# Sliding-window attention on 32-row array tiles: scores of two heads with 64 keys per tile, full PSUM banks, static probability buffers and a hand-made order of all array work

## The chip, the cores and the metric

One core of one Trainium2 chip runs the whole program. The metric is the device time of one execution in microseconds (us). Every run is compared with runs of the kernel before on the same chip.

Engines: PE is the matmul array (PEld its weight loads), DVE is VectorE, ACT is ScalarE, POOL is GpSimd, SP issues most transfers. Each executes its own list of instructions in order (the VectorE timeline of e6 below shows one standing behind another); semaphores tie them together.

## The reference

Two layers, each an attention block and a feed-forward block with residuals, 2048 rows of 512, 32 heads of 16, a window of 256 keys:

```python
def _A_ref(x, wqkv, wo):
    H = 32; Dh = D // H; W = 256
    # ... q, k, v from x @ wqkv
    scores = jnp.einsum("bhqd,bhkd->bhqk", q, k) * (Dh ** -0.5)
    mask = (idx[:, None] - idx[None, :] >= 0) & (idx[:, None] - idx[None, :] < W)
    p = _softmax(jnp.where(mask, scores, -1e9))
    # ... o = p @ v, then o @ wo
x = x + _A_ref(_layernorm(x), A_wqkv, A_wo)
x = x + _B_ref(_layernorm(x), B_w1, B_w2)    # relu feed-forward, 512 -> 1792 -> 512
# ... and both once more
```

## The kernel before

Rows are worked on in four chunks of 512 per layer. The scheduler of the build orders all instructions by five priority classes (scores first, feed-forward last). Q is isolated per head by transfers into zero-padded tiles, so that one matmul over all 128 rows of K gives the scores of four heads; GpSimd masks, and GpSimd computes the layer-norm rows:

```python
def layer_norm_chunk(c, xnT, sfx, startup=False, j0=0, j1=4):
    # ... statistics on VectorE; rstd by Ln and Exp on ScalarE
    nc.vector.scalar_tensor_tensor(out=nb[:, j0:j1], in0=mv4[:, j0:j1, 0], scalar=-1.0, in1=rstd[:, j0:j1],
                                   op0=ALU.mult, op1=ALU.mult)
    # ... for each of four row blocks
            nc.gpsimd.tensor_scalar(out=xn[:], in0=x_sb[:, b, :], scalar1=rstd[:, j:j + 1],
                                    scalar2=nb[:, j:j + 1], op0=ALU.mult, op1=ALU.add)
            nc.sync.dma_start_transpose(out=xnT[...], in_=xn[...])

# scores of one block of 128 queries with one block of 128 keys, eight heads
for xh in range(2):
    nc.tensor.matmul(Sps[:, xh]..., lhsT=KT[:, t, kcols], rhs=Qih[:, t, 4 * xh:4 * xh + 4, qcols], start=True, stop=True)
nc.scalar.activation(pt[:, kbi]..., Sps[...], ACT.Exp)
# ... two masks on GpSimd (affine_select), then 8 heads x 3 key blocks:
nc.tensor.matmul(acc[:, h % 16, :], lhsT=pt[:, kbi, j, :], rhs=Vaug[:, slot(layer, kb), h, :], ...)
```

## Time and profile before

| | before |
|---|---|
| time, median (range) | 643.74 us (641.53 to 643.77) |
| span in the profile, mean granted clock of the array | 643.3 us, 0.970 |
| busy: PE, DVE, ACT, POOL | 576, 321, 368, 368 us |

The lines that carry the bound stand in the prediction below. In the page's table of groups the columns are line, engine, operation, out<-in, shapes, count, then busy us and mean ns of one, then the engine's idle time just before and what ended most of it.

### The profile page before, as it was taken

How to read it: one execution, taken by the hardware profiler on the slowest of the kernel's cores; microseconds unless marked ns; L12 is line 12 of the kernel's file. 1: busy time of each engine (PE TensorE's matmuls, PEld its weight loads, DVE VectorE, ACT ScalarE, POOL GpSimd, SP SyncE). 2: the span in 40 equal slices, each digit the busy share in tenths (PEclk: the TensorE clock that was granted, in tenths of full speed). 3: DMA queues.
4: the chain of work that ended last, by engine and by line, in shares of the span. 5: the costliest groups of instructions: out<-in, count | busy, mean ns of one | idle time of the engine just before them, and what ended most of it. 6: DMA issues, size and time to landing. Idle time of an engine off the chain costs nothing.

```text
span 643.3 us, 12352 instructions
## 1 busy us (share of the span) xinstructions
PE 576.2 (90%) x5053; PEld 282.8 (44%) x5053; DVE 321.1 (50%) x701; ACT 368.2 (57%) x407; POOL 367.7 (57%) x391
## 2 busy tenths in 40 slices
PE   6957979999989999999899999999998899979994
PEld 2323434544544444534453444534454344534442
DVE  2794533544465634476455634475443544436361
ACT  5667686999850399705870399705894079920000
POOL 2168778888861287815872287814887147851200
PEclk8968996999999999999999999999999999999998
DMA  9601121111002110102101110202102210131302
GB/s 316 202 22 34 31 55 42 26 34 43 10 9 42 45 31 10 43 8 50 34 11 41 42 34 11 42 10 52 23 10 57 36 25 9 19 59 16 58 8 39
DMA packets 69217, 27.10 MB, mean 42 GB/s; under 512 B 52512, under 2 KB 68640, under 8 KB 69152
## 3 DMA queue, kind: packets, MB, share of 16 engines
q1 hardware_dynamic: 63984, 19.94, 13.6%
q0 software_dynamic: 2304, 2.10, 2.2%
q10 hardware_dynamic: 2864, 4.19, 1.8%
q8 instruction: 41, 0.67, 0.5%
q14 instruction: 24, 0.20, 0.1%
HBM read 7.86 MB, written 2.10 MB: 15 GB/s over the span
## 4 chain that ended last, share of the span: by engine, by line
PE 32%; POOL 19%; DMA 11%; issue 10%; ACT 8%; DVE 4%; SPq 0%; POOLq 0%; ACTq 0%
DMA OT<-O 9%; ACT pt L225 8%; PE ps_d L353 7%; POOL pt L228 7%; PE Sps L223 5%; PE ps_d L346 5%; POOL O L259 4%; POOL pt L232 4%; PE ps_w L333 3%; PE ps_d L176 3%; PE acc L240 3%; PE ps_d L184 3%; PE ps_d L191 3%; POOL O L257 2%; DMA xn2T<-xnB 1%
## 5 line engine op out<-in xcount | busy, mean ns | idle before, releaser
L225 ACT ACTIVATE pt<-Sps 128x1024 bf16<-128x1024 f32 x360 | 344.8, 1025 | 95.3 <-PE Sps L223 82.8
L223 PE MATMUL Sps<-Qi,KT 128*128 128x512 bf16 x720 | 218.9, 386 | 4.1 <-ACT pt L225 2.8
L228 POOL TENSOR_SCALAR_AFFINE_SELECT pt<-pt 128x1024 bf16<-128x1024 bf16 x128 | 140.3, 1099 | 67.4 <-ACT pt L225 67.1
L232 POOL TENSOR_SCALAR_AFFINE_SELECT pt<-pt 128x1024 bf16<-128x1024 bf16 x112 | 122.2, 1091 | 34.4 <-ACT pt L225 31.4
L240 PEld LDWEIGHTS <-pt 128*128 128x128 bf16 x2880 | 100.2, 96 | 87.6 <-POOL pt L228 38.4
L240 PE MATMUL acc<-Vaug,pt 128*128 128x17 bf16 x2880 | 108.9, 171 | 26.4 <-POOL pt L228 20.7
L346 PE MATMUL ps_d<-xn2T,w 128*128 128x512 bf16 x448 | 123.9, 378 | 0.9 <-DVE hT L348 0.9
L348 DVE TENSOR_SCALAR hT<-ps_d 128x512 bf16<-128x512 f32 x112 | 77.1, 689 | 61.4 <-PE ps_d L346 61.0
L353 PE MATMUL ps_d<-w,hT 128*128 128x512 bf16 x448 | 105.7, 381 | 0.0
L223 PEld LDWEIGHTS <-KT 128*128 128x128 bf16 x720 | 64.3, 97 | 68.5 <-issue 16.8
L334 DVE TENSOR_TENSOR x_sb<-ps_w,x_sb 128x512 f32<-128x512 f32 x32 | 22.1, 692 | 102.2 <-PE ps_w L333 80.8
L353 PEld LDWEIGHTS <-hT 128*128 128x128 bf16 x448 | 43.2, 98 | 50.4 <-issue 1.9
L346 PEld LDWEIGHTS <-w 128*128 128x128 bf16 x448 | 39.8, 97 | 43.2 <-issue 5.7
L333 PE MATMUL ps_w<-wo,OT 128*128 128x512 bf16 x128 | 38.3, 390 | 18.4 <-DMA OT<-O 18.3
L162 POOL TENSOR_SCALAR xnB<-x_sb,rstdB,nbB 128x512 bf16<-128x512 f32 x32 | 24.4, 766 | 42.4 <-DMA xn2T<-xnB 25.5
L247 DVE RECIPROCAL chk<-acc 128x16 f32<-128x16 f32 x64 | 16.4, 256 | 56.8 <-PE acc L240 56.7
L162 POOL TENSOR_SCALAR xnA<-x_sb,rstdA,nbA 128x512 bf16<-128x512 f32 x28 | 21.4, 769 | 40.2 <-DVE nbA L150 37.7
L178 DVE CAST QT<-ps_d 128x512 bf16<-128x512 f32 x32 | 22.0, 689 | 37.2 <-PE ps_d L176 37.2
L147 ACT ACTIVATE lnvB<-mv4B,ln_bias 128x4 f32<-128x4 f32 x8 | 2.4, 296 | 66.2 <-DVE mv4B L143 66.2
L357 POOL DMA_DIRECT2D out_dram<-x_sb x16 | 9.1, 570 | 52.8 <-DVE x_sb L355 37.2
L176 PE MATMUL ps_d<-xnT,wqkv 128*128 128x512 bf16 x128 | 36.4, 399 | 2.6 <-DVE QT L178 1.8
L355 DVE TENSOR_TENSOR x_sb<-ps_d,x_sb 128x512 f32<-128x512 f32 x32 | 22.0, 689 | 28.4 <-PE ps_d L353 25.8
(62 smaller groups left out, 391.5 us busy)
## 6 DMA issues: line engine op xcount, KB each, us to landing
Qi<-QT SPq DMA_DIRECT2D x128, 32.0 KB, 2.0
w<-in_B_w_dram ACTq DMA_DIRECT2D x2, 1792.0 KB, 13.9
xst<-in_A_x_dram SPq DMA_DIRECT2D x4, 512.0 KB, 14.4
out_dram<-x_sb POOLq DMA_DIRECT2D x16, 128.0 KB, 2.3
wqkv<-in_A_wqkv_dram SPq DMA_DIRECT2D x3, 512.0 KB, 13.1
wo<-in_A_wo_dram ACTq DMA_DIRECT2D x1, 512.0 KB, 5.5
OT<-O SPq DMA_TRANSPOSE x32, 2.3
xn2T<-xnB SPq DMA_TRANSPOSE x32, 2.4
```

Source lines behind the costliest of these rows:

```text
L162: nc.gpsimd.tensor_scalar(out=xn[:], in0=x_sb[:, b, :], scalar1=rstd[:, j:j + 1], scalar2=nb[:, j:j + 1], op0=ALU.mult, op1=ALU.add)
L176: nc.tensor.matmul(ps[:], lhsT=wqkv[:, kc, t * P:(t + 1) * P], rhs=xnT[:, kc, :], start=(kc == 0), stop=(kc == KC - 1))
L223: nc.tensor.matmul(Sps[:, xh].rearrange("p j q -> p (j q)"), lhsT=KT[:, t, kcols], rhs=Qih[:, t, 4 * xh:4 * xh + 4, qcols], start=True, st ...
L225: nc.scalar.activation(pt[:, kbi].rearrange("p j q -> p (j q)"), Sps[:].rearrange("p x j q -> p (x j q)"), ACT.Exp)
L228: nc.gpsimd.affine_select(out=pt[:, 2], in_=pt[:, 2], pattern=[[0, 8], [1, P]], compare_op=ALU.is_ge, fill=0.0, base=0, channel_multiplier=-1)
L232: nc.gpsimd.affine_select(out=pt[:, 0], in_=pt[:, 0], pattern=[[0, 8], [-1, P]], compare_op=ALU.is_gt, fill=0.0, base=0, channel_multiplier=1)
L240: mm = nc.tensor.matmul(acc[:, h % 16, :], lhsT=pt[:, kbi, j, :], rhs=Vaug[:, slot(layer, kb), h, :], start=(ii == 0), stop=(ii == len(kbi ...
L259: nc.gpsimd.tensor_tensor(out=O3, in0=O3, in1=ok[:].to_broadcast([P, 32, 16]), op=ALU.mult)
L333: nc.tensor.matmul(ps[:], lhsT=OT[:, kc, :], rhs=wo[:, kc, :], start=(kc == 0), stop=(kc == KC - 1))
L346: nc.tensor.matmul(ps[:, n0:n1], lhsT=w1[:, kc, f * P:(f + 1) * P], rhs=xnT[:, kc, n0:n1], start=(kc == 0), stop=(kc == KC - 1))
L348: nc.vector.tensor_relu(hT[:, f, n0:n1], ps[:, n0:n1])
L353: nc.tensor.matmul(ps[:], lhsT=hT[:, f, j * P:(j + 1) * P], rhs=w2[:, f, :], start=(f == 0), stop=(f == NF - 1))
```

## The change

Intent: stream fewer score columns. A 32-row tile of the array holds K of two heads, 64 keys each, so that the product fills 128 output rows; four such tiles work side by side, and the masks are meant to cost less because the blocks are 64 wide. Probabilities lie in two static buffers, and every array instruction is put in one fixed order by a dependency on the one before. Layer norm is rewritten too: rstd comes from a power operation on GpSimd, and the row becomes (x - mean) * rstd.

```diff
+    def in_order(inst):
+        if chain[0] is not None:
+            tc.add_manual_dep(inst.ins, chain[0].ins.name, NOSYNC, reason="array order")
+        chain[0] = inst
...
-        nc.scalar.activation(lnv[:, j0:j1], mv4[:, j0:j1, 1], ACT.Ln, bias=ln_bias[:], scale=LN_PRESCALE)
-        nc.scalar.activation(rstd[:, j0:j1], lnv[:, j0:j1], ACT.Exp, bias=exp_bias[:], scale=-0.5)
-        nc.vector.scalar_tensor_tensor(out=nb[:, j0:j1], in0=mv4[:, j0:j1, 0], scalar=-1.0, in1=rstd[:, j0:j1], ...)
+        nc.gpsimd.tensor_tensor(out=rstd[:, j0:j1], in0=rstd[:, j0:j1], in1=mhalf[:, j0:j1], op=ALU.pow)
-        nc.gpsimd.tensor_scalar(out=xn[:], in0=x_sb[:, b, :], scalar1=rstd[:, j:j + 1],
-                                scalar2=nb[:, j:j + 1], op0=ALU.mult, op1=ALU.add)
+        nc.gpsimd.tensor_scalar(out=xn[:], in0=x_sb[:, 4 * c + j, :], scalar1=mv[:, j, 0:1],
+                                scalar2=rstd[:, j:j + 1], op0=ALU.subtract, op1=ALU.mult)
...
+        for kb, lo, n, at in blocks:
+            for r in range(4):
+                rows = slice(32 * r, 32 * r + 32)
+                mm(Sps[r // 2][:, r % 2, 64 * at:64 * (at + n)], KBD[rows, t, sl, :],
+                   Qt[rows, 64 * lo:64 * (lo + n)], True, True)
...
+            nc.vector.tensor_tensor(out=v, in0=v, in1=m, op=ALU.min)     # masks of 3 groups of 5; 2 stay on GpSimd
...
+                        nc.vector.tensor_copy(V2[64 * e:64 * e + 64, sl, :, 17 * e:17 * e + 16],
+                                              v4[64 * half:64 * half + 64, :, e, :])
...
+        at_slot(SPS * k + 5, begin)       # layer norm of the next chunk; its projections from slot SPS * k + 8
```

A slot is one of 160 steps of the order: a group of scores, then about nine long matmuls and a fifth of the PV work of the unit before (PV is the product of probabilities and V). A chunk is 20 slots. The probability buffers alternate from unit to unit.

## The prediction

> **What bounds the kernel now.** I read the table of engines first, then busy time by stretch, then the order of array work in a middle stretch, then the waits of the array between 100 and 600 us.
>
> ```profile
> span 643.3 us, 12352 instructions
> PE 576.2 (90%) x5053; PEld 282.8 (44%) x5053; DVE 321.1 (50%) x701; ACT 368.2 (57%) x407; POOL 367.7 (57%) x391
> ...
> L225 ACT ACTIVATE pt<-Sps 128x1024 bf16<-128x1024 f32 x360 | 344.8, 1025 | 95.3 <-PE Sps L223 82.8
> L223 PE MATMUL Sps<-Qi,KT 128*128 128x512 bf16 x720 | 218.9, 386 | 4.1 <-ACT pt L225 2.8
> ```
>
> The array (PE) is the only engine near its span, but busy does not mean streaming: a matmul's 0.38 us includes the depth of the pipeline. The real cost of one is the step from one to the next. The timeline gives it:
>
> ```profile
> 313.74 0.73 PE L240 MATMUL acc<-Vaug,pt 128*128 128x17 bf16 x23
> ...
> 622.32 12.25 PE L353 MATMUL ps_d<-w,hT 128*128 128x512 bf16 x56
> ```
>
> 56 matmuls of 512 columns last 12.25 us, the last of them 0.38: (12.25-0.38)/55 = **0.216 us** each. 23 probability-times-V matmuls of 17 columns last 0.73, the last 0.17: (0.73-0.17)/22 = **0.0255 us** each; their width hardly counts, so wider ones should cost the same. So the array's necessary work is 2128 of the first kind (720 scores, 448+448 feed-forward, 512 projections) = 460 us, plus 2880 x 0.0255 = 73 us: 533 us of 643.
>
> ```profile
> 28.00:100.00 72.00, 54.61 (x556) 26.30 (x555) 43.28 (x105) 51.51 (x61) 51.85 (x54) 0.88 0.17 38
> 100.00:600.00 500.00, 464.87 (x4249) 231.81 (x4249) 250.91 (x546) 300.39 (x330) 306.65 (x317) 0.99 0.14 29
> ...
> PE ps_w L333 <- DMA OT<-O: 17.0, 25, 2.3
> PE acc L240 <- POOL pt L228: 14.2, 26, 1.4
> ```
>
> (Columns of the first two: window, length, then busy time and count of PE, PEld, DVE, ACT, POOL, then granted clock.) In the 500 us there are 1754 long matmuls and 2495 short ones: 379+64 = 443 us of streaming. The other 57 us, 11%, are waits, the named ones on the transposed O and on the mask that GpSimd applies. So the kernel is bound by array work with a tenth lost in waits; the first 28 us do hardly any attention.
>
> **What the Trainium skill says.** (1) "TensorE: Matmul & The Clock Gate", Back-to-back issue gap: N/2.4 + 2.5 ns when warm, never under about 25 ns. The trace agrees: 216 ns at 512 columns, 25.5 at 17. (2) The same page, Measured speedup vs the span model: four row tiles with K=32, N=512 ran 3.07 times as fast as one after the other. No tiled matmul is in the trace before. (3) "TensorEngine Tiling (Array Packing)", Key Properties: changing the tiling mode drains the array. Nothing in the trace shows that cost either; it is my largest unknown. (4) "VectorE: DVE Perf Modes", What auto-detection actually checks: a two-tensor operation on 16-bit operands of unit step runs at two elements a cycle. No such operation on VectorE is in the trace before.
>
> **The change, part by part**, with counts from the order of the two built programs, main path only.
>
> Scores. Before, each 32-row stretch of K meets a zero-padded Q over all 128 rows: 720 x 0.216 = 156 us. After, 1408 matmuls of 64 to 320 columns, each on a 32-row tile, in 352 groups of four; two heads of 64 keys fill the 128 output rows, so only needed queries are streamed. Their columns sum to 307,200. One at a time that is 307,200/2.4 GHz = 128 us; divided by 3.07, 42 us (the issue floor is 1408 x 0.0255 = 36 us). The array enters and leaves tiled mode once in each of 160 slots. A lone short matmul takes 0.17 us from start to end, so I put a drain between 0 and 0.17 us and choose 0.06: 320 x 0.06 = 19 us. Scores: 61 us, **95 less**.
>
> Other array work. The 1408 long matmuls stay (304 us). The 2880 PV matmuls now have 34 columns but keep their count and step (73 us). Array floor 438 us instead of 533.
>
> ScalarE. 360 exponentials become 304: 272 of 1024, 16 of 640, 16 of 512 columns. In a run they follow each other in 0.955 us (9.55 us for ten), so about 260+22+9 = 291 us.
>
> VectorE. It takes over most masks and more complicated evacuations. From durations before (0.689 us for 512 columns from PSUM, 0.416 for 256): relu 112 = 77, Q copies 32 = 22, K written twice with zeros (48 of 512, 32 of 256) = 46, V in 128 quarter copies of 256 = 53, normalizing 64 x (0.256+0.416) = 43, residual adds 64 = 44, layer-norm statistics and the rest about 70, and 152 masks at an estimated 0.42 (407 cycles at 0.96 GHz, from page (4)) = 63. About **418 us against 321**.
>
> GpSimd. 240 masks of about 1.1 us, and the two operations per block that clip O (33.5+19.8 us), go; 368 small masks of 256 elements come. Between 128 elements (0.291 us) and 1024 (1.099) a line gives 0.41: 150 us. With the layer-norm rows about 220 us, off the path. The 128 small transfers that isolated Q go too.
>
> Order. Each slot is scores, about 9 long matmuls and a fifth of the previous unit's 96 PV matmuls, in fixed order. PV uses probabilities made a unit earlier, and O's transposes get two slots, so both waits named above should vanish in the middle.
>
> The sum along the array. Ordinary slot: scores 0.41 + 9 x 0.216 + 19 x 0.0255 = 2.84 us. ScalarE needs per slot two exponentials, 1.91, plus the scores between them, 0.41, because a slot takes both score buffers, plus about 0.2 of handover: 2.5 us. So the array leads in the ordinary slots and ScalarE in some 35 thin ones, where no projection is ready (2.5 us; 2.0 in the first chunk of a layer, whose windows are cut). Over the slots: 43+51+55+5x57 = 434 us. Start: scores at about 20 us instead of 26, since Q is not isolated by transfers. End, after the last scores: the order holds 138 long and 115 short matmuls there, 33 us, plus 12 us for the last normalize, transpose and layer norm, plus the 9 us that the end takes after the last matmul before: 54. Together 508 us. Then waits on VectorE: in each of seven projection stages, four K/Q rounds of 2.07 us and four V rounds of 1.66 make 15 us, with masks and norms 19, against 15 of array time, and only two PSUM buffers in between: 4 us each, 28 us. Copies queued behind a mask that waits for its exponential: about 4. **Prediction 540 us.**
>
> **Rivals.**
> A: VectorE becomes the bound. Its 418 us lie in about 460 us of slots, 90%, in strict order, and the projection slots exceed the array. For it: 0.689 us copies behind two buffers. Against: 0.05 to 0.1 us of neighbouring short operations overlap in the trace, and the second feed-forward matmul has one evacuation per 14 matmuls. If it lags everywhere: 570 to 590.
> B: The row tiles do not overlap, or each switch drains fully. No overlap adds 86 us: about 620. A full 0.17 us drain adds 35: 575. For it: page (3), and nothing measured here. Against: page (2), and each tile has its own bank.
> C: ScalarE becomes the bound at 2.5 us a slot or more, the exponential being slower into rows of 576: then all slots take 2.6 to 2.9 and nothing is lost beyond some 10 us.
> D: Hand-made order is perfect and drains cost nothing: about 490 to 505.
>
> **Range and chances.** D gives the low end, 505; A and half of B together the high end, 590. Only serial tiles with VectorE lag come near 643, so faster by over 2% has 0.95, within 2% 0.03, slower 0.02.
>
> **What would show it.** Right: scores' four-tile groups last about 0.3 us for 512 columns in each row; PV steps stay at 0.026; slots of about 2.85 us; array waits named after VectorE evacuations in projection stages, none after O's transposes or GpSimd masks in the middle; VectorE busy near 400. Wrong: score groups near 0.85 us (B), VectorE busy above 90% through feed-forward slots (A), or ScalarE without idle in ordinary slots (C). An unexpected wait of the fixed order, say on the layer-norm chain three slots ahead of its projections (about 8.5 us for four rows), would add up to 5 us in each chunk and break the high end.

## More of the kernel before

```profile
L162 POOL TENSOR_SCALAR xnB<-x_sb,rstdB,nbB 128x512 bf16<-128x512 f32 x32 | 24.4, 766 | 42.4 <-DMA xn2T<-xnB 25.5
L162 POOL TENSOR_SCALAR xnA<-x_sb,rstdA,nbA 128x512 bf16<-128x512 f32 x28 | 21.4, 769 | 40.2 <-DVE nbA L150 37.7
```

Here the reader sees 60 operations of 0.77 us, 46 us in all, on an engine with idle time around them.

## The result, and the profile after

The changed kernel took 679.38 us (677.07 to 681.31), the kernel before 642.91 us beside it: **slower by 5.4%** (95% interval 4.9 to 5.9). Ratios in this document are made from fast runs of the same rounds, so not quite the ratio of the medians quoted, which here would be 5.7%. The prediction was 540 us.

The page of the changed kernel: spans, busy time by engine, and the rows that answer to those shown of before.

```profile
span 675.3 us, 13941 instructions
PE 501.4 (74%) x5741; PEld 235.2 (35%) x5741; DVE 392.9 (58%) x914; ACT 295.2 (44%) x323; POOL 326.8 (48%) x505
...
L251 ACT ACTIVATE Pb<-Sps 128x1024 bf16<-128x1024 f32 (+2 forms) x320 | 292.7, 968 | 301.4 <-PE Sps L93 186.4
L93 PE MATMUL Sps<-Qt,KBD 32*128 32x320 bf16 (+4 forms) x1408 | 71.4, 267 | 18.5 <-ACT Pb L251 16.8
L182 POOL TENSOR_SCALAR xnB<-x_sb,mvB,rstdB 128x512 bf16<-128x512 f32 x32 | 67.0, 2097 | 1.8 <-DMA xn2T<-xnB 0.2
L182 POOL TENSOR_SCALAR xnA<-x_sb,mvA,rstdA 128x512 bf16<-128x512 f32 x28 | 57.8, 2071 | 8.4 <-DMA xnT<-xnA 7.7
```

The array's busy time fell by 75 us, yet the span grew: the array now stands idle. Its mean granted clock fell too, from 0.970 to 0.878. No engine is full. The layer-norm rows, the same 60 with the same shapes, take 2.1 us in place of 0.77. Who the array waited for (waiter, what it waited for, us in total, times, longest):

```profile
PE ps_d L93 <- DMA xnT<-xnA: 71.8, 6, 17.3
PE ps_d L93 <- DMA xn2T<-xnB: 21.3, 2, 14.7
PE Sps L93 <- ACT Pb L251: 16.8, 34, 0.7
PE ps_d L93 <- DVE V L232: 13.5, 32, 0.8
PE ps_d L93 <- DVE KBD L215: 10.7, 21, 1.0
PE ps_d L93 <- DMA OT<-O: 9.3, 4, 4.9
```

Eight waits, all on the transposed layer-norm rows, make 93 us. Where nothing is late, a slot looks as hoped. The array's timeline near the end (start us, length us, what):

```profile
599.31 0.40 PE L93 MATMUL Sps<-Qt,KBD 32*128 32x256 bf16 x8
599.64 1.25 PE L93 MATMUL ps_d<-w,hT 128*128 128x512 bf16 x5
600.73 0.66 PE L93 MATMUL acc<-V,Pb 128*128 128x34 bf16 x20
601.23 1.24 PE L93 MATMUL ps_d<-w,hT 128*128 128x512 bf16 x5
602.40 0.40 PE L93 MATMUL Sps<-Qt,KBD 32*128 32x320 bf16 x8
```

Eight score tiles hold the array for 599.64-599.31 = 0.33 us, and the slot lasts 3.09 us; the prediction's own terms give 0.41 + 10 x 0.216 + 20 x 0.0255 = 3.08. So the slot costs what I summed, though not term by term: of the two stretches of five long matmuls, the one before PV takes 600.73-599.64 = 1.09 us and the one before scores 602.40-601.23 = 1.17. The last long matmul before scores holds the array longer; the part on what held comes back to it. Now one of the waits, from the timelines of GpSimd, of the SP queue and of the array, put in order of time:

```profile
427.23 4.13 POOL L182 TENSOR_SCALAR xnA<-x_sb,mvA,rstdA 128x512 bf16<-128x512 f32 x2
...
486.53 1.93 PE L93 MATMUL ps_d<-xnT,wqkv 128*128 128x512 bf16 x7
486.94 0.71 POOL L175 TENSOR_TENSOR rstdB<-rstdB,mhalf 128x2 f32<-128x2 f32 x1 [5.98 <-DVE rstdB L174]
487.76 4.14 POOL L182 TENSOR_SCALAR xnB<-x_sb,mvB,rstdB 128x512 bf16<-128x512 f32 x2
...
489.87 4.09 SPq L184 DMA_TRANSPOSE xn2T<-xnB  x2
...
494.06 7.87 SPq L184 DMA_TRANSPOSE xnT<-xnA  x4
496.59 4.12 POOL L182 TENSOR_SCALAR xnA<-x_sb,mvA,rstdA 128x512 bf16<-128x512 f32 x2 [4.08 <-DMA xnT<-xnA]
...
503.32 1.01 PE L93 MATMUL ps_d<-xnT,wqkv 128*128 128x512 bf16 x2 [9.39 <-DMA xnT<-xnA]
```

Read it downward. The first two xnA rows, for the next projections, are ready at 431, 63 us before anything transposes them: their target xnT has one buffer, and the last projections of the chunk before read it until 488. Two rows for the feed-forward part (xnB) hold GpSimd for 4.14 us, their transposes leave the one SP queue first, and the four for xnT follow at 494.06. The last two xnA rows cannot be written until the first two have been transposed (there are two row buffers), take another 4.12 us, and at 503.32 the array resumes after 9.39 us in which it did nothing. Its next instruction in the pinned order was a projection, and little else was ready: the feed-forward work of the five chunks before was done (280 matmuls of each half), and GpSimd starts on the last rows of the sixth only at 504.31.

The other chunks look alike. The first transpose into xnT starts 0.4 to 6.0 us after the start of the last projection that reads the old one; in the last five chunks the first two rows had then been ready for 62 to 90 us. At each of the six waits the array asks for the new xnT 1.6 to 5.9 us after that last read, and from the first transpose until it resumes 9 to 17 us pass.

### The profile page after: what moved, and what is told of

It reads as the page before. It is cut to its first block, busy times and chain, and to the rows that moved or that the text cites. A ratio compares the mean times of both kernels' runs of the same rounds, so it can differ in the third digit from the quotient of the medians.

```text
span 675.3 us, 13941 instructions
## 1 busy us (share of the span) xinstructions
PE 501.4 (74%) x5741; PEld 235.2 (35%) x5741; DVE 392.9 (58%) x914; ACT 295.2 (44%) x323; POOL 326.8 (48%) x505
## 4 chain that ended last, share of the span: by engine, by line
PE 40%; DVE 22%; POOL 18%; issue 11%; DMA 5%; ACT 3%; SPq 0%; POOLq 0%; ACTq 0%
PE ps_d L93 30%; DVE V L232 8%; POOL xnB L182 7%; PE acc L93 6%; PE Sps L93 4%; DVE KBD L215 4%; POOL xnA L182 4%; POOL Pb L257 3%; DVE Pb L271 3%; ACT Pb L251 3%; DMA xnT<-xnA 3%; DMA OT<-O 2%; POOL rstdB L175 1%; DVE stB L171 1%; DVE x_sb L339 1%
## 5 line engine op out<-in xcount | busy, mean ns | idle before, releaser
L251 ACT ACTIVATE Pb<-Sps 128x1024 bf16<-128x1024 f32 (+2 forms) x320 | 292.7, 968 | 301.4 <-PE Sps L93 186.4
L257 POOL TENSOR_SCALAR_AFFINE_SELECT Pb<-Pb 64x256 bf16<-64x256 bf16 x368 | 153.3, 417 | 208.7 <-ACT Pb L251 190.3
L93 PEld LDWEIGHTS <-Pb 128*128 128x128 bf16 x2880 | 95.8, 97 | 44.7 <-issue 11.7
L93 PE MATMUL acc<-V,Pb 128*128 128x34 bf16 x2880 | 98.6, 179 | 2.4 <-POOL Pb L257 2.1
L93 PE MATMUL Sps<-Qt,KBD 32*128 32x320 bf16 (+4 forms) x1408 | 71.4, 267 | 18.5 <-ACT Pb L251 16.8
L271 DVE TENSOR_TENSOR Pb<-Pb,tri 128x512 bf16<-128x512 bf16 (+1 forms) x152 | 60.1, 425 | 35.4 <-ACT Pb L251 34.6
L182 POOL TENSOR_SCALAR xnB<-x_sb,mvB,rstdB 128x512 bf16<-128x512 f32 x32 | 67.0, 2097 | 1.8 <-DMA xn2T<-xnB 0.2
L182 POOL TENSOR_SCALAR xnA<-x_sb,mvA,rstdA 128x512 bf16<-128x512 f32 x28 | 57.8, 2071 | 8.4 <-DMA xnT<-xnA 7.7
L232 DVE CAST V<-ps_d 64x256 bf16<-64x256 f32 x128 | 54.0, 422 | 2.1
L215 DVE TENSOR_SCALAR KBD<-ps_d,par 128x512 bf16<-128x512 f32 (+1 forms) x80 | 47.2, 634 | 11.6 <-PE ps_d L93 11.6
```

The lines of the kernel that those rows point to most:

```text
L93: inst = nc.tensor.matmul(o, lhsT=lhsT, rhs=rhs, start=start, stop=stop)
L182: nc.gpsimd.tensor_scalar(out=xn[:], in0=x_sb[:, 4 * c + j, :], scalar1=mv[:, j, 0:1], scalar2=rstd[:, j:j + 1], op0=ALU.subtract, op1=ALU ...
L215: nc.vector.tensor_scalar(out=KBD[:, t, sa:sa + b - a, 64 * e:64 * e + 64], in0=ps[0][:, 64 * a:64 * b].rearrange("p (s k) -> p s k", k=64 ...
L232: nc.vector.tensor_copy(V2[64 * e:64 * e + 64, sl, :, 17 * e:17 * e + 16], v4[64 * half:64 * half + 64, :, e, :])
L251: nc.scalar.activation(pv4[:, 2 * rp:2 * rp + 2, 64 + a:64 + z], Sps[rp][:, :, a:z], ACT.Exp, scale=0.25)
L257: nc.gpsimd.affine_select(out=v, in_=v, pattern=[[0, 4], [-1 if far else 1, 64]], compare_op=ALU.is_gt if far else ALU.is_ge, fill=0.0, ba ...
```

## The experiments

Four theories. **1**: the row operation is slow on GpSimd. **2**: the chain starts too late in the fixed order, with one xnT buffer, whatever the operation takes. **3**: VectorE's evacuations behind two PSUM buffers, the rival of the prediction. **4**: pinning the array order is a cost of its own.

Times are medians; the kernel before ran at 643 to 644 us beside each batch. The last column compares with the kernel before.

| run | what | us | ratio (95%) |
|---|---|---|---|
| | the change | 679.4 | 1.054 (1.049 to 1.059) |
| e1_mult_add | rows as x*rstd + nb | 642.8 | 0.998 (0.994 to 1.003) |
| e2_mult_subtract | rows as x*rstd - mean*rstd | 686.4, one run | |
| e4_early_rows | rows earlier, two buffers | 614.7 | 0.954 (0.949 to 0.959) |
| e5_three_psum | 3+1 PSUM buffers, not 2+2 | 714.9 | 1.111 (1.106 to 1.117) |
| e11_before_slow_row | kernel before with the slow row | 687.4 | 1.067 (1.061 to 1.073) |
| e9_free_order | the change, order not pinned | 649.3 | 1.010 (1.005 to 1.015) |
| e6_early_and_mult_add | e1 and e4 | 600.6 | 0.934 (0.929 to 0.938) |
| e13_v_half_on_act | e6, half of V copies on ScalarE | 612.6 | 0.950 (0.943 to 0.956) |
| e12_split_end | e6, last feed-forward split | 600.0 | 0.930 (0.923 to 0.937) |
| e15_more_masks_on_pool | e6, one mask group to GpSimd | 611.0 | 0.948 (0.941 to 0.955) |
| e16_split_end_more_pool | e12 and e15 | 609.8 | 0.946 (0.938 to 0.953) |
| e17_nb_on_pool | e6, nb on GpSimd | 591.4 | 0.919 (0.915 to 0.922) |
| e18_repaired_free_order | e6, order not pinned | 582.0 | 0.905 (0.902 to 0.907) |
| e19_nb_on_pool_free_order | e17, order not pinned | 573.3 | 0.892 (0.888 to 0.896) |

All gave the right result.

### First batch: which cause

e1_mult_add changes the operation alone.

```diff
+        nc.vector.scalar_tensor_tensor(out=nb[:, j0:j1], in0=mv[:, j0:j1, 0], scalar=-1.0, in1=rstd[:, j0:j1],
+                                       op0=ALU.mult, op1=ALU.mult)
-            nc.gpsimd.tensor_scalar(out=xn[:], in0=x_sb[...], scalar1=mv[:, j, 0:1],
-                                    scalar2=rstd[:, j:j + 1], op0=ALU.subtract, op1=ALU.mult)
+            nc.gpsimd.tensor_scalar(out=xn[:], in0=x_sb[...], scalar1=rstd[:, j:j + 1],
+                                    scalar2=nb[:, j:j + 1], op0=ALU.mult, op1=ALU.add)
```

> The changed kernel, with the layer-norm rows computed as x*rstd + nb (nb = -mean*rstd from one small VectorE operation) in place of (x - mean)*rstd; nothing else. Theory 1, the row operation itself: GpSimd's subtract-then-multiply took 2.1 us a row where multiply-then-add took 0.77; rows fall back to about 0.77 us, the array's waits on the transposed rows fall from 93 us to under 40, the clock rises above 0.92, the time falls to 595-620 us. Theory 2, the place of the chain in the fixed order (it may start only three slots ahead and has one buffer): rows get fast but the array still waits over 60 us on them; 640-660 us. Theory 3, VectorE's evacuations behind two PSUM buffers: little changes, within 15 us of 679.

Measured 642.8 us, 37 us less than the change and level with the kernel before. The group of rows and the first wait of the array in this run:

```profile
L189 POOL TENSOR_SCALAR xnB<-x_sb,rstdB,nbB 128x512 bf16<-128x512 f32 x32 | 25.2, 797 | 5.2 <-DVE nbB L179 3.0 <-DMA xn2T<-xnB 1.7 <-DVE mvB L174 0.3
...
PE ps_d L93 <- DMA xnT<-xnA: 41.0, 6, 8.7
```

Rows are back at 0.8 us and the waits on rows fell from 93 to 55 us (41.0 and 13.6). The time lies in theory 2's range (640-660), the waits between the two (under 40 and over 60): the operation explains 37 us, and a late chain remains. From the first transpose until the array resumes it still takes 8 to 10 us in the last five chunks.

e4_early_rows keeps the slow operation and starts it nine slots earlier.

```diff
-        at_slot(SPS * k + 5, begin)
+        at_slot(max(5, SPS * k - 4), begin)
-        xnTs[k] = work.tile([P, KC, 512], BF16, name="xnT", tag="xnT", bufs=1)
+        xnTs[k] = work.tile([P, KC, 512], BF16, name="xnT", tag="xnT", bufs=2)
-        OT = work.tile([P, KC, P], BF16, name="OT", bufs=4)
+        OT = work.tile([P, KC, P], BF16, name="OT", bufs=3)
```

(Q tiles 6 to 5, and a constant of 256 bytes moved, for space.)

> The changed kernel with the slow row operation kept, but the rows of the next chunk begun nine slots earlier in the recorded order and two buffers for their transpose (paid for by 3 instead of 4 buffers of transposed O and 5 instead of 6 of Q). Theory 1: GpSimd has enough idle time, so an earlier start hides most of the slow rows in the middle, waits on these rows fall from 72 us to under 25, but the 14.7 us wait at the end stays; 600-625 us. Theory 2: the same fall, and more of it than from a faster operation. Theory 3: within 15 us of 679.

Measured 614.7 us, 65 us less, with rows still at 2.1 us. The wait on xnT has left the list of the nine longest; the 14.7 us at the end stay, and GpSimd's masks are waited for in three places (11.6 us), since slow rows stand in front of them. So both theories hold, and this edit is worth more than the operation. It changes two things, the slot and the second xnT buffer, and no run tries them apart. The trace of the change speaks for the buffer, since its first rows were ready 62 us and more before they could be transposed; here the first transpose of chunks 4 to 6 follows 2.1 us after its row begins.

e5_three_psum gives evacuations a third buffer and takes one from the PV accumulator.

```diff
-ps_acc bufs=2, ps_d bufs=2
+ps_acc bufs=1, ps_d bufs=3
```

> The changed kernel with three buffers for projection and feed-forward results and one for the PV accumulator, in place of two and two. Theory 3, evacuations on VectorE behind two buffers: the 31 us that the array waits on them fall to under 12 us and the time falls to about 655. Theories 1 and 2: these waits fall a little, but the array reaches the same layer-norm waits sooner, so the time falls by under 10 us; the single accumulator costs a few us.

A miss for every theory: 714.9 us. The waits on V copies fell to 9.8 us, but the single accumulator is now waited for:

```profile
PE acc L93 <- DVE O L281: 50.9, 29, 3.5
```

The run cannot decide theory 3, since it bought evacuation buffers with a dearer one. It shows that the second accumulator is needed.

e11_before_slow_row puts the slow operation into the kernel before and changes nothing else.

```diff
-                nc.gpsimd.tensor_scalar(out=xn[:], in0=x_sb[:, b, :], scalar1=rstd[:, j:j + 1],
-                                        scalar2=nb[:, j:j + 1], op0=ALU.mult, op1=ALU.add)
+                nc.gpsimd.tensor_scalar(out=xn[:], in0=x_sb[:, b, :], scalar1=mv4[:, j, 0:1],
+                                        scalar2=rstd[:, j:j + 1], op0=ALU.subtract, op1=ALU.mult)
```

> The kernel before, with its 60 layer-norm rows after the start computed by GpSimd as (x - mean)*rstd, as the change does, and nothing else. Theory 1: each row takes about 2.1 us here too, so the cost belongs to the operation and not to its neighbours; its array order is not pinned, so other work fills the gap and only a part of 60 x 1.33 = 80 us shows: 650-685 us. Rival: the rows are slow in the changed kernel for another reason (contention with VectorE for memory, say), and stay at 0.77 us here; 643 us.

```profile
L162 POOL TENSOR_SCALAR xnB<-x_sb,mv4B,rstdB 128x512 bf16<-128x512 f32 x32 | 66.3, 2076 | 43.7 <-ACT rstdB L148 23.9 <-DMA xn2T<-xnB 19.7
...
PE acc L240 <- POOL pt L228: 48.9, 39, 5.3
```

The same 2.08 us a row in another kernel with other neighbours: the cost belongs to the operation. It cost this kernel 44 us, in the main through the masks that queue behind the rows on GpSimd (20.7 us of such waits in the whole run before, 48.9 in this one). Those 28 us are not all; the array also ran longer at half the clock, and by the estimate of the fourth batch lost 27 us to it in place of 9, which would cover the rest. With like rows, the rest of the change is thus a little better than the kernel before (679 against 687), and with fast rows level (643 against 643): its array saving is eaten elsewhere.

### Second batch: what in the operation, and does the order itself cost

e2_mult_subtract replaces the addition by a subtraction of mean*rstd.

```diff
-        ... scalar=-1.0 ...   op0=ALU.mult, op1=ALU.add
+        ... scalar=1.0 ...    op0=ALU.mult, op1=ALU.subtract
```

> As the multiply-then-add version of the changed kernel, but multiply-then-subtract (x*rstd - mean*rstd): one look at what makes the row slow. If the subtraction is what GpSimd does slowly, these rows take about 2.1 us as well and the time is near 679; if the slow thing is multiplication as the second of the two operations, or the operand that comes from the statistics tile, they take about 0.77 and the time is near 643.

The rows of this run, from the view of one tile (count, duration in ns as min/median/max):

```profile
L189 POOL TENSOR_SCALAR xnA<-x_sb,rstdA,nbA x28: 2067/2076/2119, 28.0 to 508.5; 128x512 bf16<-128x512 f32 x28
```

Same operands, same shapes as e1; only `add` became `subtract`, and a row takes 2.08 us again. On GpSimd the two pairs with a subtraction are slow, first or second, and the pair without is fast. Why is not shown.

e9_free_order leaves the order of the array to the build's scheduler.

```diff
-    chained = [True]
+    chained = [False]
```

> The changed kernel with the pinning of the array order switched off, so that the scheduler of the build orders the array work (slow rows and late start kept). Theory that pinning turns a late row into an idle array: the built order now sets other work before the late projections, the waits on transposed rows fall from 93 to 50-70 us, and the time lies at 650-670; the rest stays because the scheduler too has to finish attention in time. Rival, that the hand-made order is sound and only the chain behind it is late: 675-700, since feed-forward work that fills the gaps is missing later and scores are split into more stretches.

```profile
PE acc L93 <- POOL Pb L257: 41.2, 8, 10.9
PE ps_d L93 <- DMA xnT<-xnA: 23.3, 5, 8.3
PE ps_d L93 <- DMA xn2T<-xnB: 14.4, 1, 14.4
```

649.3 us, 30 us less than the pinned order and just below the range of theory 4, with rows as slow. Waits on rows fell to 38 us, but PV now waits 41.2 us for masks (2.1 in the change): rows and masks together 79 us in place of 95. The short waits fell by more: on exponentials from 16.8 to 4.5 us, on V copies from 13.5 to 4.5, on K copies from 10.7 to 2.8, 29 us in all. So free order helps, as theory 4 says, but only in part by hiding late rows; whether it helps when nothing is late is left to e18.

e6_early_and_mult_add is e1 and e4 together.

> Both repairs of the layer-norm chain in the changed kernel: multiply-then-add rows, and the next chunk's rows begun nine slots earlier with two buffers. Theory 1+2, that the chain of rows is the whole difference to the prediction's sum: waits of the array on transposed rows of the projections vanish, those at the end fall to about 11 us, GpSimd masks are no longer waited for, and the time falls to 590-605 us; the clock to above 0.91. What would remain above my 540 is then the evacuations (about 30 us of waits, which the prediction had) and the clock. If another cause lies behind, such as ScalarE setting the slots, it stays above 610.

600.6 us, as expected of both; xnT is no longer among the waits and the clock rose to 0.928. Both repairs are needed: 37 and 65 us alone, 79 together.

e13_v_half_on_act tests theory 3 properly, by taking copies from VectorE.

```diff
-                        nc.vector.tensor_copy(V2[...], v4[...])
+                        (nc.scalar.copy if e else nc.vector.tensor_copy)(V2[...], v4[...])
```

> Both repairs, and in addition half of the quarter copies of V (64 of 128) on ScalarE in place of VectorE. If VectorE's evacuations behind two buffers are the next thing (theory 3), waits on V copies fall from some 13 us to under 5 and the time by 8 to 15 us against the version with both repairs. If ScalarE, which then has 64 more operations of about 0.45 us, delays scores instead, waits on its exponentials rise by as much and the time stays within 5 us.

```profile
PE ps_d L93 <- ACT V L239: 23.9, 22, 3.2
```

12 us slower than e6, a miss for both forecasts: the waits on exponentials stayed at 17.9 us. The V copies stand behind exponentials in ScalarE's strict order, and the array waits 23.9 us for them, up to 3.2 us at a time, where it had waited 15.9 us on VectorE's. ScalarE's copies also stood 19.1 us behind VectorE's copies of the same tile, so the halves ran one after the other. And the array ran longer at half clock: by the estimate of the fourth batch 32 us lost in place of 21. Here a less busy engine was no help.

### Third batch: the end and the masks

e12_split_end lets the last feed-forward start on half of its rows.

```diff
+            if k == NSTEP - 1:
+                box["i"] = w1_items(..., 0, 256) + w1_items(..., 256, 512)
```

> Both repairs, and the first feed-forward half of the very last chunk cut in two: 56 matmuls of 256 rows' columns for the first two row blocks, then 56 for the last two. Theory: the 11.1 us that the array waits at the end are the last rows' layer norm with nothing else to do; the first half can start on rows that are ready, so that wait falls to about 4 us and the time by 5 to 10 us, against about 600 with both repairs. Rival: the first half's rows come as late as the second's (same GpSimd and transfer queue), and nothing is won.

A miss in its sum: 600.0 us, the same. The long wait at the end shrank from 11.1 to 7.6 us, but 112 matmuls of half width took 17.15 us where e6's 56 of full width took 15.08 (one of them is missing from its trace).

e15_more_masks_on_pool and e16_split_end_more_pool move one mask group from VectorE to GpSimd.

```diff
-    POOL_GROUPS = (1, 2)
+    POOL_GROUPS = (1, 2, 3)
```

> Both repairs, and the masks of one more of the five groups on GpSimd (three groups in place of two): VectorE loses 64 operations of about 0.43 us, GpSimd gains 256 of 0.42. Theory 3 again, that evacuations wait because VectorE is full and stands behind masks: array waits on V, K, Q and residual copies fall from 45 to about 35 us, the time by 5 to 12 us from 600. If these waits come only from two copies per four matmuls, and not from how much else VectorE does, they stay and so does the time (within 4 us).

> The two together. If both help by what is expected of each, 580 to 590 us; if neither does, 600.

Both missed: 611.0 and 609.8 us, 10 us worse than without. The copies of V were waited for 10.6 us instead of 15.9, but PV began to wait for GpSimd's masks (6.2 us) and the sum of all waits between first and last scores stayed (72.5 and 73.1 us, e6 and e15). What grew is the time at half clock outside the waits: by the estimate of the next batch 30 us lost in place of 21, about the 10 us. Why the clock was low for longer is not shown.

### Fourth batch: what was left above the prediction

In e6 one wait of the array is 2.35 us on a residual addition. VectorE's timeline explains it, with the array's line last:

```profile
163.11 0.20 DVE L176 TENSOR_SCALAR rstdA<-mvA 128x4 f32<-128x4 f32 x1
164.89 0.16 DVE L179 SCALAR_TENSOR_TENSOR nbA<-mvA,rstdA 128x4 f32<-128x4 f32 x1 [1.59 <-POOL rstdA L177]
164.97 0.68 DVE L346 TENSOR_TENSOR x_sb<-ps_d,x_sb 128x512 f32<-128x512 f32 x1
...
165.71 1.87 PE L93 MATMUL ps_d<-wo,OT 128*128 128x512 bf16 x4 [2.35 <-DVE x_sb L346]
```

The tiny nb operation of my own repair waits for GpSimd's power; the residual addition that would free a PSUM buffer stands behind it; the array stands behind that. After the wait four matmuls take 1.87 us where four take 1.04 in a running stream: the granted clock is 0.50 in this stretch. In all these traces it is recorded as either 1.0 or 0.5. Adding up, between first and last scores and outside waits of over 0.15 us, half of the time at 0.5 gives an estimate of what the array lost to the clock, if it works half as fast then, as 1.87 against 1.04 suggests: 9 us in the kernel before, 29 in the change, 21 in e6.

e17_nb_on_pool removes the round trip.

```diff
-        nc.vector.scalar_tensor_tensor(out=nb, in0=mean, scalar=-1.0, in1=rstd, op0=ALU.mult, op1=ALU.mult)
+        nc.vector.tensor_scalar(out=nb, in0=mean, scalar1=-1.0, scalar2=None, op0=ALU.mult)   # before the power
+        nc.gpsimd.tensor_tensor(out=nb, in0=nb, in1=rstd, op=ALU.mult)                        # after it
```

> Both repairs, with nb = -mean*rstd finished on GpSimd (mean negated by VectorE beforehand) so that VectorE no longer waits in order for GpSimd's power operation. Theory: in the version with both repairs one wait of the array, 2.35 us on a residual addition, comes from a residual standing behind nb on VectorE, which waits 1.59 us for rstd; there are 23 such nb operations. VectorE's waits on rstd (about 19 us) vanish, array waits on VectorE's copies and residuals fall by 5 to 10 us, and the time falls to 590-596 from 600. Rival: GpSimd's extra operation lengthens the chain as much; within 4 us of 600.

591.4 us, 9 us less, as expected; waits on this residual addition fell from 7.0 to 4.3 us, with a longest of 0.8.

e18_repaired_free_order and e19_nb_on_pool_free_order switch the pinning off in e6 and e17.

> Both repairs, with the pinning of the array order switched off. With slow rows, switching it off won 30 us. Theory that pinning only costs where something is late: with the rows on time it now wins little or loses, 595-610 us against 600. Rival that pinning itself costs, whatever the rows do: again some 25 us faster, near 575.

> nb on GpSimd and the order not pinned, together: if the two effects add, the difference to the pinned version with nb on GpSimd equals that of the pair before; expected 590-605 us.

582.0 and 573.3 us, the second better than its forecast of 590-605. My theory that pinning costs only where something is late has fallen: with the rows on time it still costs 18.6 and 18.1 us, about 60% of the 30 it cost with slow rows. In between my two forecasts, nearer to the rival. The effects add: nb on GpSimd is worth 9.2 us pinned and 8.7 free. The best version, e19, by its page and its waits:

```profile
span 568.5 us, 14014 instructions
PE 499.6 (88%) x5741; PEld 239.4 (42%) x5741; DVE 394.2 (69%) x939; ACT 295.4 (52%) x323; POOL 254.3 (45%) x530
...
PE ps_d L93 <- DMA xn2T<-xnB: 11.1, 1, 11.1
PE ps_d L93 <- DMA OT<-O: 9.5, 3, 4.1
PE ps_d L93 <- DVE KBD L222: 8.5, 14, 2.4
PE acc L93 <- POOL Pb L264: 5.7, 3, 3.1
```

It beats both kernels: 0.892 of the kernel before, 106 us less than the change as given. Its waits on scores' buffers (ScalarE) are 2.8 us in place of 18.0 in e6, and those on V copies 5.4 in place of 15.9: my reading, not tested apart, is that free order lets the array do something else in the thin slots and the projection slots. The loss to the clock, by the estimate above, is 10 us in e18 and 15 in e19.

## Why the prediction was wrong, point by point

**The step that failed** is the sentence on GpSimd: "With the layer-norm rows about 220 us, off the path." I took a row's price from the kernel before, 0.77 us, although the diff replaces its operation pair. It measured 2.1 us, and GpSimd was busy 327 us: 60 rows x 1.3 us more are 79, and 25 power operations, which I had not priced, another 20. Above all it was not off the path. I had named the danger ("on the layer-norm chain three slots ahead of its projections (about 8.5 us for four rows)") and bounded it at 5 us a chunk; six waits of up to 17.3 us, 72 in sum, and 21 more on the feed-forward rows were measured. The 8.5 us were not far off for fast rows (8 to 10 in e1), but with slow ones it is 9 to 17. What was wrong in either case is "three slots ahead": one xnT buffer holds the chain until the chunk before has read it, and the array asks for the next 1.6 to 5.9 us later. e1, e2 and e11 show the price, e4 the chain (slot and buffer together), e6 the two together: 79 us.

**The second failed step** is the sum of the slots. Even with both repairs (e6) the time from first to last scores is 537.7-23.6 = 514 us, where I had 434 and 32 of waits. Of the 48 us that were missing, the trace of e6 gives about 40. Waits on VectorE's copies and residuals are 45 us and not 32. The array loses about 21 us to half clock, the estimate above, for which I had nothing. Scores with their switches cost about 6 us more than I had (see "What held"). This overlaps with what runs won back: the nb round trip that my repair added, 9 us (e17), and pinning, 18 us (e18).

**Start and end.** First scores came at 24.5 us, not 20; from the last scores to the end it took 63.7 us, not 54, of which 14.7 are the wait for the last layer norm (11.1 with fast rows).

**What held.** The tiles overlap: 512 columns in each of four row stretches hold the array 0.33 us, where one after the other would take four times 0.216, 2.6 times as long (I had divided by 3.07), so rival B's serial tiles are out. The drain I had too small. In the trace of the change the last long matmul before scores holds the array 0.312 us in place of 0.215 (medians at full clock, 132 places; in the kernel before it is 0.215 before scores too), and the 0.33 are 0.11 above 0.216 of streaming: together 0.21 us a slot where I had 0.12. Scores thus cost about 67 us in 160 slots and not 61, an estimate at full clock: 0.10 us, and 0.32 as the mean of the 118 undisturbed slots, some of which have fewer columns. PV of 34 columns: 96 in 2.56 us of which the last 0.18, so 0.025 each. VectorE: 393 us in place of 418, a mask 0.434 in place of 0.42, a V copy 0.422 in place of 0.416. ScalarE: 295 in place of 291. A GpSimd mask: 0.417 in place of 0.41. Waits on evacuations: 13.5 for V, 12.2 for K, 3.7, 2.8 and 0.6 for residuals, feed-forward and Q, 33 us in place of 32. Rival A was thus sized rightly for the change (45 us in e6) but is not what decided; e13 and e15, which tried to relieve VectorE, made things worse. Rival C is seen only in thin slots, 16.8 us of waits on exponentials.

**Slips in the working.** The "other 57 us" between 100 and 600 us were not all shown to be waits: the waits that the view lists there sum to 34. And 540 with rival B's 86 us is 626, not 620.

**The chances** were the worst error: 0.95 for faster, with a named failure whose size rested on one unpriced operation.

## What to carry to other kernels

Price every operation that a diff touches, also where it "only" rewrites algebra: two formulas for one value can differ 2.7 times on one engine. Look for the last reader of every single buffer: what is to be written there next cannot start before, however early it is put in the order. A pinned order makes the latest producer the bound of everything behind it, so each producer needs slack in slots and in buffers before the order is fixed, and a scheduler's order may still be better. When a small operation on one engine waits for another engine, look at what stands behind it in the same queue.

## What the Trainium skill lacked or had wrong

- "GPSIMD Engine Reference", Elementwise — side-by-side cycle accounting, gives 768 ns for 512 elements in the best case, which the multiply-and-add row meets (766 and 769 ns before). It does not say that the pair matters: with a subtraction, as first or second operation, the same row took 2071 to 2097 ns on average in three kernels (the change, e2, e11).
- No page gives a price for the power operation on GpSimd: here it took 0.73 us for 128x2 elements and 1.03 us for 128x4.
- "TensorEngine Tiling (Array Packing)", Key Properties, says that a mode switch drains the array and gives no number. Here the last long matmul before row tiles holds the array 0.10 us longer, and 8 to 12 row tiles with 512 columns in each row stretch hold it 0.33 us, 0.11 above streaming: 0.21 us for entering and leaving together, issue included.
